# Keeping network products together between attention steps in the planned order of a fused attention and feed-forward kernel

## The chip, the cores and the metric

The kernel runs on one core of a Trainium2 chip. The metric is the device time of one execution in microseconds (us); before the change its median over 3 runs is 943.97 us (943.89 to 944.54).

## What is computed

Attention over q, k, v of 4 batches, 8 heads, 576 tokens and 64 columns, in two parts that are added: a softmax attention over tokens averaged in fours (its output repeated four times), and a local one in which a token sees tokens fewer than 4 places away. Its output, as 2304 tokens by 512 columns, goes through two feed-forward networks. The reference, cut:

```python
out_d = sm_attn(q_d, k_d, v_d)              # q, k, v averaged over 4 tokens
out_up = np.repeat(out_d, factor, axis=2)
scores = np.where(abs(i - j) < factor, scale * q @ k.T, -1e9)
attn_out = out_up + softmax(scores) @ v
g = x @ w_gate                              # 512 -> 1536
y = (g * sigmoid(g)) * (x @ w_val) @ w_out  # 1536 -> 512
h = np.maximum(y @ w_in, 0.0)               # 512 -> 2048
return h * h @ w_out2                       # 2048 -> 512
```

## The kernel before

Every engine executes its instructions in the order in which the program wrote them, and that order is not written by hand. A planner (class `Order`, its `run` and `next`) holds queues of tasks; a task is a chain of stages, each with an engine, a cost in planned us, the buffers that it takes and gives back, and a condition. The planner keeps a planned clock for each engine, looks which stages could start, and writes the instructions of the one that it picks (`s.fn()`), moving that engine's clock on. The chip then waits by semaphores wherever the plan was too early.

TensorE (PE) has two kinds of work.

**Attention steps.** Local attention has scores (L649, with L644 adding the mask in the first two batches), a transpose of the probabilities (L686) and the product with v (L707). Pooled ("global") attention has scores (L797), transposes (L816) and the product with v (L835). Between scores and transpose VectorE (DVE) and ScalarE (ACT) make a softmax; the transposed block is copied by ACT; the last product is read by ACT (L852) or added into a tile of x by DVE (L725). All of them write one of four PSUM banks with the tag `att`, used in turn. L649, L707, L797 and L835 use part of the 128 rows and columns of the array (the trace names them 64\*64, 64\*72 or 72\*64, and counts two records for each one of the program); L644 and L686 use 128\*128, L816 uses 72\*72.

**Network products.** A step is 12 matmuls of 128x128 weights with 256 tokens: four blocks of the depth, each as three products of high and low halves (`three`, L1045 to L1047). A unit of the first network is three steps, gate and value (into the two `gv` banks) and down (into `y`). Between value and down stands a chain: DVE L1094 multiplies, ACT L1100 makes the high half, DVE L1103 the low half of `hh`, which down reads. The second network follows, with products of blocks (L1045 to L1047 and L1980 to L1982), after all attention is done. The weights come in by DMA as raw bits and are taken apart by ACT and DVE (L367 to L384, L423, L426), in between.

Which kind PE takes next is decided in `next`: among PE's stages that could start within `LOOK_T` of the earliest, `rank` prefers attention (rank 0) to network products (rank 1) until attention steps in a row (`streak`) have used `ATT_MAX` planned us; then network products come first (rank -1). Attention stages are given `PE_MARGIN` of 0.1 us more than their inputs need.

Where a PE step that takes a bank is planned to wait over 0.6 us and the planned clock is between 40 and 100 us (or the step is a network product), `fill_bank` sets `pad`, and `bank` (L81) writes that many matmuls on zeros into the bank ahead of the step. Up to 40 us such matmuls are written by `fill` (L1251).

Of the kernel before, what the change touches and what calls it, by code (L numbers as in the profile page):

```python
# [63 lines left out]
def attn_moe_kernel(ctx: ExitStack, tc: tile.TileContext, qT, kT, vw, vin, vp, qp, kp, qs, ks, vs, maskc, masks, identc, wB, wC, out):  # L64
# [33 lines left out]
    def dma(size):  # L98
        return size / RATE

    AFTER = {"v": 0.15, "a": 0.2, "p": 0.2, "t": 0.25}
    ATT_MAX, LOOK_V, LOOK_A, LOOK_P, LOOK_T, LOOK_D, PE_MARGIN = 2.0, 0.1, 0.0, 0.2, 0.05, 0.6, 0.1
    PAD_END, PAD_WAIT, PAD_SHARE = 100.0, 0.6, 0.8
    TICK, FILL_END, BUSY = 10.24 / 3, 40.0, 3180
    W_DUE0, W_STEP, X_DUE0, X_STEP, X_STEP0 = 17.0, 2.2, 12.0, 20.0, 14.0
    S_DUE, S_STEP = 140.0, 15.0
    CUT_T, CUT_J, W_LAG, Q_LATE, Q_LATER, MASK_PE = 2, 4, 65.0, 10.0, 6.0, 2
    V_LATE, V_LATE1, V_LATE0, V_LEAD, W_LEAD, LEAD, LATE = -15.0, -10.0, -5.0, 1000.0, 1000.0, 80.0, 500.0
# [4 lines left out]
    class Stage:  # L113
        def __init__(self, engine, cost, fn, take=(), give=(), cond=None, share=1.0, late=0.0):
            self.engine, self.cost, self.fn, self.take, self.give, self.cond = engine, cost, fn, take, give, cond
            self.share, self.late = share, late
# [14 lines left out]
    class Order:  # L131
        def __init__(self):
            self.flying = []
            self.queues = {k: [] for k in ("x", "qk", "sum", "rows", "v", "att", "w", "mlp", "other", "done", "put")}
            n = {"att": N_ATT, "y": N_Y, "gv": N_GV, "p": N_P, "pt": N_PT, "v": N_V, "xt": N_XT}
            n |= {"sg": N_SG}
            self.free = {k: [0.0] * c for k, c in n.items()}
            self.named = {k: [(0.0, i) for i in range(n_[0])] for k, n_ in NAMED.items()}
            self.got = {k: [] for k in NAMED}
            self.clock = {e: 0.6 for e in "vaptd"}  # L140
            self.pad = 0
            self.load, self.filler, self.streak, self.landed = {}, None, 0.0, 0.0

        def hot(self, t):
# [59 lines left out]
        def next(self):  # L204

            found = {}
            heads = [(q[0], q) for q in self.queues.values() if q]
            for task, q in [(t, None) for t in self.flying] + heads:
                t = self.start(task)
                if t is None:  # L210
                    continue
                e = task.stages[task.at].engine
                if e is None:
                    return task, q, t, None
                wait = PE_MARGIN if e == "t" and not task.products else 0.0
                found.setdefault(e, []).append((max(t + wait, self.clock[e]), task, q, t))
            assert found, "no stage can go on"
            first = min(found, key=lambda e: min(c[0] for c in found[e]))
            limit = min(c[0] for c in found[first]) + LOOK[first]

            def rank(c):
                task = c[1]
                if task.products:
                    return (1 if first == "t" and self.streak < ATT_MAX else -1), task.due
                return 0, task.due

            _, task, q, t = min((c for c in found[first] if c[0] <= limit), key=rank)
            return task, q, t, first

        def run(self):  # L230
            while self.flying or any(self.queues.values()):
                task, q, t, engine = self.next()
                if q is not None:
                    q.pop(0)
                    self.flying.append(task)
                if task.at == 0:
                    self.flying += task.then
                s = task.stages[task.at]
                if engine == "t" and (task.products or self.clock["t"] >= FILL_END) and self.clock["t"] < PAD_END:
                    self.fill_bank(t, s)  # L240
                for k in s.take:
                    if k in self.named:
                        slot = min(self.named[k])
                        self.named[k].remove(slot)
                        self.got[k].append(slot[1])
                    else:
                        self.free[k].remove(min(self.free[k]))
                if engine == "t" and self.clock["t"] < FILL_END:
                    self.fill(max(t, self.clock["t"]), task)
                s.fn()  # L250
                if engine is not None:
                    c, cost = max(t, self.clock[engine]), s.cost
                    if engine == "t":
                        cost = self.columns(c, cost, s.share)
                        self.streak = 0.0 if task.products else self.streak + cost
                    self.clock[engine] = c + cost
                    t = c + cost + AFTER.get(engine, 0.0) + s.late
                    if engine == "d":

                        t = self.landed = max(c + FLIGHT, self.landed) + cost  # L260
                        self.clock["d"] = max(c + ISSUE, self.landed - AHEAD)
                        t += SLACK if c > FIRST else 0.3
                    if engine == "p":

                        self.landed = max(c + FLIGHT, self.landed) + dma(128 * HP * SD) * ACC
                        self.clock["d"] = max(self.clock["d"], self.landed - AHEAD)
                        t = max(t, self.landed + SLACK)
                task.ready = t
                task.times.append(t)
                task.at += 1  # L270
                for k in s.give:
                    if callable(k):
                        name, slot = k()
                        self.named[name].append((t, slot))
                    else:
                        self.free[k].append(t)
                if task.done:
                    self.flying.remove(task)
# [2164 lines left out]
```

## Time and profile before

| | |
|---|---|
| median of 3 runs | 943.97 us (943.89 to 944.54) |
| the profiled execution | 943.21 us, of which 941.4 us from the first to the last instruction |
| PE matmul busy | 931.3 us, 99% of the span, 8929 instructions |
| DVE busy | 758.2 us, 81% |
| ACT busy | 583.4 us, 62% |
| DMA | 183.82 MB, 195 GB/s on average |

Busy is the time in which an engine had at least one instruction; matmuls overlap, so PE can be busy all the time and still not start matmuls at its fastest. What a step costs is therefore read from the distance between the starts of two steps in the timeline. The chain of waits that ended last lies on PE for 96% of the span.

### The profile page before, as it was taken

The numbers are of one execution on the slowest core, as the hardware profiler recorded it, in microseconds if no ns is written. First come the engines' busy times: TensorE is split into PE (matmuls) and PEld (weight loads), VectorE is DVE, ScalarE is ACT, GpSimd is POOL, SyncE is SP. The second block draws the span as 40 slices with busy tenths as digits, with TensorE's granted clock in tenths as the row PEclk, the third lists the DMA queues.
The fourth block names the chain that finished last, engine by engine and source line by source line (L and its number), as shares of the span: only waits on it lengthen the run. The fifth ranks groups of instructions, "written<-read, shape, count | busy, mean of one in ns | idle before, by whom it ended". The sixth has DMA issues, their size and how long they took to land.

```text
span 941.4 us, 22569 instructions
## 1 busy us (share of the span) xinstructions
PE 931.3 (99%) x8929; PEld 906.5 (96%) x8929; DVE 758.2 (81%) x1875; ACT 583.4 (62%) x1368; POOL 23.8 (3%) x31
## 2 busy tenths in 40 slices
PE   8999999999999999999999999999999999999997
PEld 7888999999999999999999999999999999999997
DVE  7998979778977788888896999968777667786775
ACT  4878566757666888466543575757565645445553
POOL 0102102000000000000000000000000000000000
PEclk9999999999999999999999999999999999999999
DMA  9998969485788756167462638614414864516131
GB/s 303 258 292 217 255 166 261 158 295 155 254 284 279 245 177 238 65 224 223 169 210 75 235 132 316 236 74 171 146 57 179 315 228 175 180 67 247 46 134 68
DMA packets 101205, 183.82 MB, mean 195 GB/s; under 512 B 22380, under 2 KB 60012, under 8 KB 101100
## 3 DMA queue, kind: packets, MB, share of 16 engines
q1 hardware_dynamic: 97644, 174.42, 54.7%
q0 software_dynamic: 3456, 7.96, 4.8%
q8 instruction: 70, 1.15, 0.5%
q14 instruction: 35, 0.29, 0.1%
HBM read 120.75 MB, written 61.60 MB: 194 GB/s over the span
## 4 chain that ended last, share of the span: by engine, by line
PE 96%; DVE 2%; ACT 1%; issue 0%; DVEq 0%
PE gv L1045 11%; PE gv L1046 11%; PE gv L1047 11%; PE y L1045 8%; PE y L1046 8%; PE y L1047 8%; PE att L1982 6%; PE att L1981 6%; PE att L1980 6%; PE att L1046 3%; PE att L1047 3%; PE att L1045 3%; PE att L707 2%; PE att L649 2%; PE att L797 2%; PE y L1251 2%
## 5 line engine op out<-in xcount | busy, mean ns | idle before, releaser
L1045 PE MATMUL gv<-xs,wg 128*128 128x256 f32 x880 | 250.5, 285 | 0.1
L1046 PE MATMUL gv<-xs,wg 128*128 128x256 f32 x880 | 247.0, 281 | 0.0
L1047 PE MATMUL gv<-xs,wg 128*128 128x256 f32 x880 | 246.8, 280 | 0.0
L1045 PEld LDWEIGHTS gv<-xs,wg 128*128 128x128 f32 x880 | 166.2, 189 | 2.3 <-DVE sg L1089 0.4
L1047 PEld LDWEIGHTS gv<-xs,wg 128*128 128x128 f32 x880 | 166.0, 189 | 0.0
L1046 PEld LDWEIGHTS gv<-xs,wg 128*128 128x128 f32 x880 | 166.0, 189 | 0.0
L2131 ACT ACTIVATE f<-rr 128x512 fp32r<-128x512 f32 (+2 forms) x200 | 87.8, 467 | 68.2 <-PE att L1982 32.2
L1982 PE MATMUL att<-wg,f 128*128 128x256 f32 x432 | 122.5, 284 | 0.5 <-DVE f L2134 0.4
L1980 PE MATMUL att<-wg,f 128*128 128x256 f32 x432 | 121.7, 282 | 0.3 <-ACT f L2131 0.3
L1981 PE MATMUL att<-wg,f 128*128 128x256 f32 x432 | 122.0, 282 | 0.0
L2134 DVE TENSOR_TENSOR f<-rr,f 128x512 fp32r<-128x512 f32 (+2 forms) x200 | 94.6, 490 | 29.5 <-ACT f L2131 28.4
L2055 ACT ACTIVATE rr<-rr 128x512 f32<-128x512 f32 (+1 forms) x144 | 79.8, 556 | 36.8 <-DVE rr L2058 35.0
L1046 PE MATMUL y<-xs,wg 128*128 128x256 f32 x336 | 94.7, 282 | 1.1 <-DVE xs L1570 1.1
L1045 PE MATMUL y<-xs,wg 128*128 128x256 f32 x336 | 94.6, 281 | 0.0
L1047 PE MATMUL y<-xs,wg 128*128 128x256 f32 x336 | 94.3, 281 | 0.0
L1982 PEld LDWEIGHTS att<-wg,f 128*128 128x128 f32 x432 | 81.2, 188 | 1.4 <-DVE f L2134 1.3
L1980 PEld LDWEIGHTS att<-wg,f 128*128 128x128 f32 x432 | 81.8, 189 | 0.6 <-ACT f L2131 0.6
L1981 PEld LDWEIGHTS att<-wg,f 128*128 128x128 f32 x432 | 81.5, 189 | 0.0
L2140 DVE TENSOR_TENSOR rr<-rr 128x256 f32<-128x256 f32 (+1 forms) x160 | 62.6, 393 | 9.1 <-ACT rr L2055 7.1
L1046 PEld LDWEIGHTS y<-xs,wg 128*128 128x128 f32 x336 | 63.5, 189 | 1.5 <-DVE xs L1570 1.5
L1045 PEld LDWEIGHTS y<-xs,wg 128*128 128x128 f32 x336 | 63.6, 189 | 0.4 <-ACT ys L1228 0.2
L1047 PEld LDWEIGHTS y<-xs,wg 128*128 128x128 f32 x336 | 63.5, 189 | 0.0
(149 smaller groups left out, 2316.8 us busy)
## 6 DMA issues: line engine op xcount, KB each, us to landing
wst<-wB SPq DMA_DIRECT2D x36, 512.0 KB, 5.0
w_sp<-tmp SPq DMA_DIRECT2D x36, 512.0 KB, 3.6
wg<-w_sp SPq DMA_DIRECT2D x36, 512.0 KB, 4.9
wst<-wC SPq DMA_DIRECT2D x32, 512.0 KB, 5.2
y_sp<-ys SPq DMA_DIRECT2D x29, 512.0 KB, 4.5
xf_sp<-xs SPq DMA_DIRECT2D x24, 512.0 KB, 2.7
xs<-xf_sp SPq DMA_DIRECT2D x24, 512.0 KB, 5.8
ys<-y_sp SPq DMA_DIRECT2D x20, 512.0 KB, 6.8
```

The costliest lines, as they stand in the source:

```text
L649: nc.tensor.matmul(u["s"][r, c * HP + hp], q[r, hp, q0 - o : q0 - o + WIN], k[r, hp, w0 - o : w0 - o + WIN], start=not mask_pe, stop=not m ...
L707: nc.tensor.matmul(ps[rr, o : o + t1 - t0], u["v"][rr, bls[c], hpp, h2, :], pt[rr, c, hpp, h2, t0 - q0 : t1 - q0], start=True, stop=True,)
L1045: nc.tensor.matmul(o, w[:, 0], x[:, 0], start=start, stop=False, skip_group_check=more)
L1046: nc.tensor.matmul(o, w[:, 0], x[:, 1], start=False, stop=False, skip_group_check=more)
L1047: nc.tensor.matmul(o, w[:, 1], x[:, 0], start=False, stop=stop, skip_group_check=more)
L1980: nc.tensor.matmul(o, h, w[:, 0], start=first and not again and c == 0, stop=False, skip_group_check=again)
L1981: nc.tensor.matmul(o, h, w[:, 1], start=False, stop=False, skip_group_check=again)
L1982: nc.tensor.matmul(o, l, w[:, 0], start=False, stop=end, skip_group_check=again)
L2055: return lambda: nc.scalar.activation(out=whole(f, c0), in_=whole(f, c0), func=func)
L2131: nc.scalar.activation(out=fac(k, 0), in_=source(), func=AF.Copy)
L2134: nc.vector.tensor_tensor(out=fac(k, 1), in0=source(), in1=fac(k, 0).bitcast(F32), op=ALU.subtract)
L2140: go = lambda: nc.vector.tensor_tensor(out=o(), in0=a(), in1=b(), op=op)
```

## The change

The planner gets three constants and two variables. `mode` remembers the kind of PE's last step: a step of the other kind is charged `SWITCH` = 0.1 planned us. `stay` adds up the planned time of network products since the last attention step; from 100 planned us on, while it is under `STAY` = 4.0 us (three steps of 1.41), a network product ranks before attention. `ATT_MAX` goes from 2.0 to 4.0 us. Nothing that is computed changes.

```diff
-    ATT_MAX, LOOK_V, LOOK_A, LOOK_P, LOOK_T, LOOK_D, PE_MARGIN = 2.0, 0.1, 0.0, 0.2, 0.05, 0.6, 0.1
+    ATT_MAX, LOOK_V, LOOK_A, LOOK_P, LOOK_T, LOOK_D, PE_MARGIN = 4.0, 0.1, 0.0, 0.2, 0.05, 0.6, 0.1
+    SWITCH, STAY, STAY_FROM = 0.1, 4.0, 100.0
...
-            self.pad = 0
+            self.pad, self.stay, self.mode = 0, 0.0, False
...
                 if task.products:
-                    return (1 if first == "t" and self.streak < ATT_MAX else -1), task.due
+                    stay = self.stay < STAY and self.clock["t"] > STAY_FROM and self.streak == 0.0
+                    return (1 if first == "t" and self.streak < ATT_MAX and not stay else -1), task.due
...
                     if engine == "t":
+                        c += SWITCH * (self.mode != task.products)
+                        self.mode = task.products
                         cost = self.columns(c, cost, s.share)
+                        self.stay = self.stay + cost if task.products else 0.0
                         self.streak = 0.0 if task.products else self.streak + cost
```

The order of all engines moves. Lines of the kernel after the change are 5 higher (L1050 for L1045). PE has 7380 rows of instructions before and 7336 now; the 44 that are gone are 22 of the 28 fillers of L81, each a weight load and a matmul. The other PE steps are the same in number. The first 352 rows of PE and the last 5317 stand as before, and on the queue of the DMAs (SP) 28 and 201 of 368; the last attention step is among the rows that moved. Before, 57 stretches of network steps lie between attention steps, now 42.

**Around the third down step of the first network, on PE** (`gv` is written by gate and value, `y` by down). Before, in a row:

```order
L1046 MATMUL gv<-xs,wg 128x256
L1047 MATMUL gv<-xs,wg 128x256
L797 MATMUL att<-kd,qd 72x144 x4
L816 MATMUL att<-ident,p 72x72 x4
L81 LDWEIGHTS zeros
L81 MATMUL gv<-zeros 128x256
```

With the change:

```order
L1051 MATMUL gv<-xs,wg 128x256
L1052 MATMUL gv<-xs,wg 128x256
L802 MATMUL att<-kd,qd 72x144 x4
L1050 MATMUL y<-hh,wg 128x256
L1051 MATMUL y<-hh,wg 128x256
L1052 MATMUL y<-hh,wg 128x256
```

Before, 15 such fillers and then the value step follow, then L797, L707 and the down step. Now the value step stands above, and only one attention step is left between it and its down step, with no filler.

**The same place on DVE**, from the product of gate and value (`sg`) to the low half of `hh`. Before:

```order
L588 TENSOR_TENSOR p<-p,rc 72x288
L1094 SCALAR_TENSOR_TENSOR sg<-sg,gv 128x256
L379 SCALAR_TENSOR_TENSOR wf<-wst,bits 128x512
L426 TENSOR_TENSOR wg<-wf,wg 128x512
L1103 TENSOR_TENSOR hh<-sg,hh 128x256
```

With the change:

```order
L560 TENSOR_SCALAR mx<-mx 72x2
L1099 SCALAR_TENSOR_TENSOR sg<-sg,gv 128x256
L431 TENSOR_TENSOR wg<-wf,wg 128x512
L384 SCALAR_TENSOR_TENSOR wf<-wst,bits 128x512
L1108 TENSOR_TENSOR hh<-sg,hh 128x256
```

Two passes over weights stand inside this chain in both orders.

**In the third batch's attention, on PE.** Before, in a row:

```order
L1047 MATMUL y<-hh,wg 128x256
L816 MATMUL att<-ident,p 72x72 x8
L649 MATMUL att<-kT,qT 64x64 x16
L835 MATMUL att<-pt,vd 64x72 x4
L1045 MATMUL gv<-xs,wg 128x256
```

With the change:

```order
L1052 MATMUL gv<-xs,wg 128x256
L840 MATMUL att<-pt,vd 64x72 x4
L821 MATMUL att<-ident,p 72x72 x4
L654 MATMUL att<-kT,qT 64x64 x16
L840 MATMUL att<-pt,vd 64x72 x4
L821 MATMUL att<-ident,p 72x72 x4
L654 MATMUL att<-kT,qT 64x64 x16
L821 MATMUL att<-ident,p 72x72 x4
L840 MATMUL att<-pt,vd 64x72 x4
L1050 MATMUL y<-hh,wg 128x256
```

Where four attention steps (L816 twice) stood between two network steps, with one network step behind them, eight stand now, with three behind; the eight use each of the four `att` banks twice.

## Rows read from the trace of the kernel before

**Rows 1.** The page: busy time by engine, and the granted clock in slices.

```profile
PE 931.3 (99%) x8929; PEld 906.5 (96%) x8929; DVE 758.2 (81%) x1875; ACT 583.4 (62%) x1368; POOL 23.8 (3%) x31
...
PEclk9999999999999999999999999999999999999999
```

**Rows 2.** Waits of PE: line and who ended it, us in total, times, longest.

```profile
PE y L1251 <- ACT zeros L1245: 2.4, 1, 2.4
...
PE att L835 <- ACT pt L822: 0.2, 1, 0.2
```

**Rows 3.** Busy time in stretches, us: PE, PEld, DVE, ACT, POOL, clock, DMA share, GB/s.

```profile
60.00:70.00 10.00, 9.98 (x115) 8.83 (x114) 9.68 (x25) 8.28 (x26) 0.00 (x0) 1.00 0.94 295
...
100.00:150.00 50.00, 49.98 (x674) 46.69 (x671) 40.71 (x109) 33.73 (x98) 6.94 (x8) 1.00 0.82 208
...
200.00:270.00 70.00, 69.91 (x906) 65.97 (x905) 60.56 (x153) 46.66 (x115) 0.00 (x0) 1.00 0.71 231
```

**Rows 4.** Timeline of PE (start us, us, engine, line), network steps among themselves.

```profile
340.49 0.28 PE L1045 MATMUL gv<-xs,wg 128*128 128x256 f32 x1
...
341.90 0.28 PE L1045 MATMUL y<-hh,wg 128*128 128x256 f32 x1
```

**Rows 5.** Timeline of PE, 129 to 136 us: both kinds by turns.

```profile
129.63 0.36 PE L1045 MATMUL gv<-xs,wg 128*128 128x256 f32 x1
...
131.23 0.47 PE L835 MATMUL att<-pt,vd 72*64 72x72 f32 x8
131.63 0.44 PE L816 MATMUL att<-ident,p 72*72 72x72 f32 x4
132.00 0.71 PE L797 MATMUL att<-kd,qd 64*72 64x144 f32 x8
132.65 0.44 PE L816 MATMUL att<-ident,p 72*72 72x72 f32 x4
132.89 0.36 PE L1045 MATMUL y<-hh,wg 128*128 128x256 f32 x1
...
134.50 0.72 PE L835 MATMUL att<-pt,vd 72*64 72x72 f32 x16
135.15 0.45 PE L816 MATMUL att<-ident,p 72*72 72x72 f32 x4
```

**Rows 6.** Timeline of PE: a network step that a transpose follows, twice.

```profile
80.76 0.38 PE L1045 MATMUL gv<-xs,wg 128*128 128x256 f32 x1
...
82.28 0.67 PE L816 MATMUL att<-ident,p 72*72 72x72 f32 x8
...
184.87 0.36 PE L1045 MATMUL y<-hh,wg 128*128 128x256 f32 x1
...
186.37 0.49 PE L686 MATMUL att<-ident,p 128*128 128x128 f32 x3
```

**Rows 7.** The chain that ended last, fillers in it: start us, us, what.

```profile
2.38 5.40 PE y L1251 x26
...
53.85 0.87 PE att L81 x7
...
61.41 1.64 PE gv L81 x15
...
68.36 0.66 PE gv L81 x6
```

**Rows 8.** Timeline of all engines, 64 to 67 us: end of a value step to its down step.

```profile
64.20 0.28 PE L1047 MATMUL gv<-xs,wg 128*128 128x256 f32 x1
...
64.52 0.42 DVE L1094 SCALAR_TENSOR_TENSOR sg<-sg,gv 128x256 f32<-128x256 f32 x1
...
65.46 0.69 DVE L426 TENSOR_TENSOR wg<-wf,wg 128x512 fp32r<-128x512 f32 x1
...
66.53 0.19 PEld L1046 LDWEIGHTS y<-hh,wg 128*128 128x128 f32 x1 [0.22 <-DVE hh L1103]
```

**Rows 9.** Timeline: local scores, and the DVE pass that sets their bank free.

```profile
145.03 1.15 PE L649 MATMUL att<-kT,qT 64*64 64x64 f32 x32
...
147.87 0.41 DVE L661 SCALAR_TENSOR_TENSOR p<-att,mask 128x256 f32<-128x256 f32 x1
```

## Prediction

> **What bounds the kernel now.** I read the page first. PE has a matmul under way for 99% of the span, at the full granted clock in every slice [rows 1]. The waits of PE say the same: after the first 2.4 us, the largest wait of the attention part is one of 0.2 us [rows 2]. So what counts is how closely PE's matmuls follow each other, and the stretches show DVE behind it with little room while attention runs: 9.68 of 10 us from 60 to 70, some 81 to 87% later [rows 3]. For PE I then went to the timeline and measured steps from start to start. A network step among its own kind takes 1.41 us [rows 4]. Between two attention steps it takes 1.60 (129.63 to 131.23) [rows 5], and 1.52 or 1.50 where a transpose (L816, L686) follows [rows 6]. So entering network work costs about 0.10, and leaving it for a step on part of the array (L649, L707, L797, L835; small steps below) another 0.08; leaving it for a transpose costs nothing. The same rows show that attention pays among itself: four L816 transposes take 0.37 when L797 follows and 0.24 when a network step does (from 131.63 and from 132.65) [rows 5], so a change from transposes to a small step costs about 0.13. A small step costs something by itself: L835 takes 0.40 with 8 records and 0.65 with 16 [rows 5], so 0.15 is per step and not per matmul.
>
> **The change, part by part.** Nothing is added or removed but 22 fillers; everything else is order. Times are against the profiled execution, 943.21 us, which lies 0.76 under the median.
>
> *1. Fewer stretches: -1.3.* I counted borders in the two orders. Entries into network work fall from 58 to 43: 15 x 0.11 = -1.65. Exits from it to a small step fall from 39 to 30: 9 x 0.08 = -0.72. But the attention steps now stand beside each other: changes from transposes to a small step rise from 14 to 21, 7 x 0.13 = +0.9, and there is one small stretch more (78 for 77), +0.15. Sum -1.3. The bounds: -0.1 if only the borders of small steps cost (their sum is 142 before and 141 now), and -2.9 if each of 15 stretches gave back the whole 1.60 - 1.41 = 0.19.
>
> The Trainium skill (TensorEngine Tiling (Array Packing), Key Properties) says that a change of tiling mode, and not a change of tile alone, drains TensorE. By that rule this term would be the -0.1. The trace agrees that the small steps' borders cost, but a step entered from and left to L686 transposes, full-array work on both sides, still takes 1.50 (from 184.87) [rows 6], so it is not the whole of it here.
>
> *2. Fillers: -2.5.* The 28 fillers of L81 take 0.87 + 1.64 + 0.66 = 3.17 us, 0.113 each [rows 7]; 22 x 0.113 = 2.5. They stood where the planner expected PE to wait; what waits come in their place is counted in 3 and 4. The bound on the other side is there, too.
>
> *3. A down step with nothing before it: +1.1.* In the changed order the third down step follows its value step after one L797 only. In the trace that chain takes 2.33 us: the value's last matmul starts at 64.20, the down step's second matmul, the first to need the low half of `hh`, at 66.53, after DVE had two passes over weights inside the chain, one of them the 0.69 of L426 [rows 8]. DVE's new order has the same two passes there. PE has to put between them 0.12 for that last matmul, about 0.75 for L797 with its border and 0.12 for the first down matmul: 1.0. So PE stands about 1.3 us; the 0.22 that the same step waits today [rows 8] goes, +1.1 net. Without the two passes the chain would be 1.3 shorter and the wait nothing; with two more passes in DVE's queue, 2.7. Behind the waiting step on PE stands all the rest of the order, so it counts in full.
>
> *4. Attention steps closer together: +0.9.* Eight in a row go round the four `att` banks twice, so a step may come to a bank that DVE has not read yet. Laying the steps' times from the rows along both orders (an estimate), I find seven places nearer to their producer than any such place before: three behind scores L649 (1.8, 1.9 and 2.1 us after their end, before at least 2.6), two behind masks L644 and transposes L686 (2.0 and 1.3, before 2.8 and 2.3), and two products right behind their transposes (0.65 and 1.28, before 1.08 and 1.56). If all waited until their old distance, that would be 4.6 us; if DVE and ACT are simply earlier, nothing. One row tells how far a release can lag: the DVE pass that frees a bank of the scores at 145.03 ends at 148.28, at least 2.1 us after the scores do [rows 9]. By that the three places of L649 wait 0.5 together; to the other four, most of which ACT releases, the less busy engine, I give a sixth of their 2.4, hence 0.9 in all.
>
> *5. The wait of L835 [rows 2] loses its place: -0.2.*
>
> At nothing I cost the rest. After the last attention step PE's 5317 rows are the same, in the same order, so what is gained by then stays gained; attention ends with 99 network steps ahead of it instead of 102. SP issues the same 368 rows; between the first 28 and the last 201 its loads of q, k, v, raw weights and its stores are moved past each other by a few places. Their cover is that the DMA engines are busy for 71 to 82% from 100 us on [rows 3]; at 60 to 70 it is 94%, and a late load there would show as a wait of L797 or of a value step. POOL's three accumulating loads of v and of pooled keys move by a place too and wait for attention steps anyway.
>
> Sum: -1.3 - 2.5 + 1.1 + 0.9 - 0.2 = -2.0: 943.21 becomes 941.2, and on the scale of the median **942.0 us**. A measurement of this kernel can tell about 0.2%, 1.9 us, from no change, so the forecast lies near that bound.
>
> **Rivals.**
>
> *Only small borders cost.* Then grouping gains 0.1 and not 1.3: 943.2 us. For it: the 0.13 that transposes pay before a small step is as much as an entry into network work, and the small borders hardly fall. Against: the 1.50 between transposes. This is also the case in which the change does not do what it says: fewer changes of kind, as many costly borders. It is what the skill's rule above would make of it.
>
> *Slower: DVE does not keep up with attention in blocks.* At the third down step two more DVE passes stand in the chain (2.7 - 0.2 = +2.5), and all seven near places wait their whole shortfall, +4.6: -1.3 - 2.5 + 2.5 + 4.6 = +3.3, 947.3 us. It decides once new waits pass 5.7 us (1.9 over the 3.8 of terms 1 and 2). For it: DVE is busy 9.68 of 10 us where the first comes [rows 3]. Against: later DVE has an eighth to a fifth of its time free, and eight steps are followed by three network steps, 4.2 us, in which it can catch up.
>
> *More is given back.* Each stretch gives 0.19 (-2.85), the fillers were all waste (-2.5), the down step waits 0.4 instead of 1.3 (+0.2), no other wait comes, and that of L835 goes (-0.2): -5.3, 938.6 us. For it: PE never waited at the fillers' ends, so they may have been longer than the waits. Against: [rows 8].
>
> *The clock falls.* An unfilled wait might cost the full clock. The first 26 fillers, behind the opening wait, took 5.40 us, 0.21 each, against 0.11 later [rows 7]: the lower of the two levels. As long a stretch again would cost 2.5: 944.5. Against: the granted clock is full everywhere else.
>
> **How the numbers follow.** Forecast 0.46, only small borders 0.17, slower 0.17, more given back 0.17, clock 0.03. Faster by over 0.2%: six tenths of the forecast's chance (its terms leave it some 1.2 us either way) and the third rival, 0.28 + 0.17 = 0.45. Slower: the second rival but for its mild end, with a little of the clock's, 0.17 rounded. The rest, 0.38, within 0.2%. The range takes in the third rival and the lower half of the slower case: 938.4 to 945.9 us.
>
> **What would show it.** L81 with 6 fillers. Network steps still 1.60 between L816 and L835, the sum of the stretches' excess over 1.41 per step lower by about 2.4 us, part of it found again in longer transposes. A wait of PE for DVE's `hh` of about 1.3 us some 60 us into the run, and waits of 0.2 to 0.5 behind scores near 155, 162 and 228 us. From the last attention step on, equal distances. The forecast is wrong if attention ends over 3 us earlier or no earlier relative to the network steps done, or if DVE's `hh` is not what PE waits for.

## The result and the profile after

The changed kernel takes 954.15 us (median of 4 runs, 953.2 to 956.0), the kernel before 943.93 us on the same chip: a ratio of 1.011 with an interval of [1.0092, 1.0128]. It is 1.1% slower; the forecast was 942.0 us and the range ended at 945.9, so both the sign and the range were wrong. The profiled execution took 953.2 us, 10.0 us more of span than the one before. Ratios leave out executions over 1.5% above the fastest of their kernel; there was one, of 2295.61 us, in the control below. (In `after`, and in the experiments made from it, lines behind the diff stand five higher: L1050 is the L1045 of before, L712 the L707.)

The page of the changed kernel: span, PE's busy time, and the granted clock in 40 slices.

```profile
span 951.4 us, 22531 instructions
...
PE 931.8 (98%) x8907; PEld 907.0 (95%) x8907; DVE 758.0 (80%) x1875; ACT 582.9 (61%) x1368; POOL 23.8 (2%) x31
...
PEclk9999999999989999999999999999999999999999
```

Against [rows 1], PE has 22 matmuls fewer (the fillers are gone, as planned) and is as long busy, but the span is longer, and one slice of the clock, the twelfth, is not full. PE's waits name the place; where before the largest wait of the attention part was 0.2 us [rows 2], there is now one of 6.0 us (waits of PE: line and who ended it, us in total, times, longest):

```profile
PE gv L1050 <- DVE sg L1099: 6.3, 2, 6.0
...
PE att L840 <- ACT pt L827: 1.7, 4, 0.8
...
PE y L1050 <- ACT hh L1105: 1.0, 1, 1.0
...
PE y L1051 <- DVE hh L1108: 0.6, 1, 0.6
```

The stretches show when (busy us of PE, PEld, DVE, ACT, POOL; then granted clock, DMA share, GB/s). First the kernel before, then the changed one, the last three rows around the long wait:

```profile
36.00:100.00 64.00, 63.75 (x846) 56.67 (x844) 59.51 (x163) 51.70 (x150) 10.38 (x12) 1.00 0.93 263
100.00:265.00 165.00, 164.82 (x2022) 155.98 (x2019) 139.01 (x365) 108.26 (x283) 9.54 (x11) 1.00 0.75 219
265.00:300.00 35.00, 35.00 (x319) 34.64 (x319) 27.60 (x60) 24.83 (x51) 0.00 (x0) 1.00 0.90 312
```

```profile
36.00:100.00 64.00, 60.99 (x840) 53.48 (x840) 59.51 (x162) 52.64 (x149) 11.28 (x13) 1.00 0.97 267
100.00:265.00 165.00, 164.12 (x1975) 155.77 (x1970) 137.72 (x364) 106.85 (x281) 8.64 (x10) 1.00 0.73 209
265.00:300.00 35.00, 29.00 (x272) 28.64 (x271) 20.51 (x43) 17.47 (x35) 0.00 (x0) 0.90 0.73 255
...
276.00:278.00 2.00, 0.40 (x2) 0.41 (x3) 2.00 (x5) 2.00 (x5) 0.00 (x0) 0.54 0.02 6
278.00:283.00 5.00, 5.00 (x25) 5.00 (x25) 4.01 (x10) 3.65 (x9) 0.00 (x0) 0.50 0.66 201
283.00:290.00 7.00, 7.00 (x62) 7.00 (x62) 4.03 (x10) 3.70 (x8) 0.00 (x0) 1.00 0.95 309
```

PE stands for 3.01 us between 36 and 100 (before 0.25), for 0.88 between 100 and 265 (0.18), and for 6.00 between 265 and 300 (0). Behind the 6.00 the granted clock is at 0.50, the lower of the two levels, until 283.

**Where the 10.0 us lie.** Two marks divide the span: the first network step and the end of the last attention step (L707, L712). Timeline of PE (start us, us, engine, line, in brackets the idle time before and what ended it), before and after:

```profile
36.25 0.38 PE L1045 MATMUL gv<-xs,wg 128*128 128x256 f32 x1
...
268.69 1.14 PE L707 MATMUL att<-pt,vw 64*64 64x58 f32 x32
269.76 0.38 PE L1045 MATMUL gv<-xs,wg 128*128 128x256 f32 x1
```

```profile
36.69 0.39 PE L1050 MATMUL gv<-xs,wg 128*128 128x256 f32 x1
...
265.10 2.08 PE L712 MATMUL att<-pt,vw 64*64 64x58 f32 x64
267.10 0.38 PE L1050 MATMUL y<-hh,wg 128*128 128x256 f32 x1
...
271.31 0.28 PE L1052 MATMUL gv<-xs,wg 128*128 128x256 f32 x1
277.60 0.58 PE L1050 MATMUL gv<-xs,wg 128*128 128x256 f32 x1 [6.00 <-DVE sg L1099]
```

Up to the first network step 0.44 us are lost; that start varies by more than this by itself (37.44 us in the kernel before without its fillers, below, whose order up to there is that of before). Between the marks lie 233.51 us with 102 network steps before and 230.41 us with 99 after; less 1.41 us for each step [rows 4] that is 89.69 and 90.82, so +1.13. From the second mark to the end there are 671.64 us before (941.4 - 269.76) and 684.30 after; less the three steps more that are then left to do (4.23) it is **+8.43**. The sum is 10.0.

**What PE waits for at 277.60.** The timeline of the other engines at that place, in the changed kernel:

```profile
266.29 0.64 DVE L730 TENSOR_TENSOR xt<-att,g 128x464 f32<-128x464 f32 x1 [1.61 <-PE att L712]
267.22 0.64 DVE L730 TENSOR_TENSOR xt<-att,g 128x464 f32<-128x464 f32 x1 [0.29 <-PE att L712]
267.78 0.68 DVE L1363 TENSOR_TENSOR tmp<-wf,tmp 128x512 fp32r<-128x512 f32 x1
275.32 1.89 DVE L1024 TENSOR_TENSOR xs<-xt,xs 128x512 fp32r<-128x512 f32 x3 [6.86 <-ACT xs L1020]
277.13 0.41 DVE L1099 SCALAR_TENSOR_TENSOR sg<-sg,gv 128x256 f32<-128x256 f32 x1
...
274.65 2.19 ACT L1020 ACTIVATE xs<-xt 128x512 fp32r<-128x512 f32 x4 [8.67 <-DMA x_sp<-xt]
...
268.49 0.32 SPq L450 DMA_DIRECT2D w_sp<-tmp x1
268.86 2.01 SPq L1211 DMA_DIRECT2D x_sp<-xt x2
```

Read it backwards. PE has two `gv` banks, and both are full; DVE L1099 frees one, but stands on DVE behind L1024, which waits 6.86 us for ACT L1020, which waits 8.67 us for a DMA. L1020 writes the high half of x for the first block behind attention, and it is the first instruction that writes into memory that attention has used: when all attention is done the planner's function `late` (L1300) releases attention's pool of buffers and opens a second one, `post`, in the same place. The first write to `post` must wait until everything that used the old pool has ended, the transfers out of it included. One buffer of the old pool is slot 5 of `tmp`, in which converted weights wait to be stored in `w_sp`; the planner may use it until attention is done (`apart("tmp", 5, turned_all)`, L1326). Its last filling is DVE L1363 at 267.78, behind the two adds L730, and its store goes out at 268.49. The profile names another store, of x to `x_sp`, issued just after it; which of the two it is, the experiments had to say.

In the kernel before the same store went out with the two at 263.58, and the first write to `post` was ACT L1354 at 270.74, which waited for DVE only:

```profile
263.58 2.05 SPq L445 DMA_DIRECT2D w_sp<-tmp x2
...
270.74 0.94 ACT L1354 ACTIVATE tmp<-wf 128x512 fp32r<-128x512 f32 x2 [1.07 <-DVE xt L725]
```

### The profile page after: what moved, and what is told of

The parts are those of the page before. It is cut to its first block, busy times and chain, and to the rows that moved or that the text cites. A ratio compares the mean times of both kernels' runs of the same rounds, so it can differ in the third digit from the quotient of the medians.

```text
span 951.4 us, 22531 instructions
## 1 busy us (share of the span) xinstructions
PE 931.8 (98%) x8907; PEld 907.0 (95%) x8907; DVE 758.0 (80%) x1875; ACT 582.9 (61%) x1368; POOL 23.8 (2%) x31
## 4 chain that ended last, share of the span: by engine, by line
PE 87%; DVE 6%; ACT 4%; DMA 1%; issue 1%; SPq 0%; DVEq 0%; ACTq 0%
PE gv L1050 10%; PE gv L1051 10%; PE gv L1052 10%; PE y L1050 8%; PE y L1051 8%; PE y L1052 8%; PE att L1987 6%; PE att L1986 6%; PE att L1985 6%; PE att L1051 3%; PE att L1052 3%; PE att L1050 3%; PE att L802 2%; PE att L712 1%; PE y L1256 1%; PE att L654 1%
## 5 line engine op out<-in xcount | busy, mean ns | idle before, releaser
L1050 PE MATMUL gv<-xs,wg 128*128 128x256 f32 x880 | 249.7, 284 | 6.5 <-DVE sg L1099 6.3
L1050 PEld LDWEIGHTS gv<-xs,wg 128*128 128x128 f32 x880 | 166.9, 190 | 8.0 <-DVE sg L1099 6.8
L1050 PE MATMUL y<-xs,wg 128*128 128x256 f32 x336 | 94.6, 281 | 0.1
L1051 PEld LDWEIGHTS y<-xs,wg 128*128 128x128 f32 x336 | 63.5, 189 | 1.5 <-DVE xs L1575 1.5
L1050 PE MATMUL y<-hh,wg 128*128 128x256 f32 x216 | 63.3, 293 | 1.0 <-ACT hh L1105 1.0
L1050 PEld LDWEIGHTS y<-xs,wg 128*128 128x128 f32 x336 | 63.6, 189 | 0.4 <-ACT ys L1233 0.3
```

What stands on the lines that cost most here:

```text
L1050: nc.tensor.matmul(o, w[:, 0], x[:, 0], start=start, stop=False, skip_group_check=more)
L1051: nc.tensor.matmul(o, w[:, 0], x[:, 1], start=False, stop=False, skip_group_check=more)
```

## The experiments

**Theory A**: the release of attention's pool waits for the last store of slot 5; PE stands 6.0 us for it, and the idle time brings the lower clock, some 2.5 us more; the rest, 1 to 1.5 us, is the attention part. **Rivals**: the stores of x are what is waited for, or x is late (B); the clock has nothing to do with the idle time (C); the attention part itself is what costs (D).

**Slot 5 given up early.**

```diff
-late_ = Task([apart("tmp", 5, turned_all), apart("bits", 1), Stage(None, 0.0, late)])
+late_ = Task([apart("tmp", 5, lambda: 0.0 if order.clock["t"] > 245.0 else None),
+              apart("bits", 1, turned_all), Stage(None, 0.0, late, cond=turned_all)])
```

Expected: 

> The changed kernel, but slot 5 of tmp (the buffer whose last store to w_sp starts late, L450) is given up from 245 us of the plan on, so that nothing written to the second pool after attention waits for a store to w_sp. Theory A (the release of the attention pool waits for the store of slot 5; PE then stands for 6.0 us and runs at half clock for 6.83 us): the wait of 6.0 us on the gv bank and the half clock go, about 954.2 - 6.0 - 2.5 = 945.7 us (944.7 to 946.7). Rival B (what is waited for is the store of x_sp, as the row of the profile names it, or x itself is late because the last two steps of L712 now stand together): the x_sp stores and the L712 steps are as they were, so the wait and the time stay, 953 to 955 us.

Measured: 945.84 us, ratio to before 1.0011 [1.0001, 1.0021]. The stretch behind attention:

```profile
266.00:290.00 24.00, 24.00 (x223) 23.93 (x220) 18.55 (x40) 17.85 (x36) 0.00 (x0) 1.00 0.95 354
```

PE does not stand at all from 266 to 290, the clock is full, and the time is the 945.7 that theory A gave. B falls in both forms: the last two L712 steps stand together here too.

**The stores of x moved behind the release.**

```diff
+def stored_x():
+    return whole() if t < NT1 - 2 else after([late_]) if whole() is not None else None
-spill_ = Task([Stage("d", dma(128 * 4 * n), spill, cond=whole)])
+spill_ = Task([Stage("d", dma(128 * 4 * n), spill, cond=stored_x)])
```

Expected: 

> The changed kernel, but the last two stores of x to x_sp (L1211) are issued only after the attention pool has been released; the last store of tmp slot 5 to w_sp stays ahead of it. Theory A: the writer of the second pool still waits for the w_sp store, PE stands for 4 to 7 us behind DVE sg L1099 and the time is 952 to 956 us. Rival B (the x_sp stores are what is waited for): the wait goes and the time is 945 to 947 us.

Measured: 953.45 us, ratio 1.0091 [1.0076, 1.0106]. Now that the stores of x are out of the way, the timeline of ACT names the other:

```profile
276.73 2.19 ACT L1020 ACTIVATE xs<-xt 128x512 fp32r<-128x512 f32 x4 [8.24 <-DMA w_sp<-tmp]
```

PE stands 5.67 us in this trace, which is of the slowest of the four executions (954.77 us). The wait belongs to the store of `tmp`; the name in the changed kernel's row was the wrong one of two stores under way at that moment.

**The wait filled.** 48 products between the second and the third gv step:

```diff
+def cover(w, x):
+    n_gv[0] += 1
+    if n_gv[0] == 69:
+        o = bank("att")[:, :256]
+        for _ in range(16):
+            three(o, w[:, :, :128], x[0][:, :, 0, :256], True, True)
...
 proj(u["g"], w_tiles[j, 0], xh_t[name, ti], n)
+cover(w_tiles[j, 0], xh_t[name, ti])
```

(and the same behind the value's `proj`). Expected: 

> The changed kernel with 48 products of 128x256 on operands that are loaded already, into a free bank of the att tag, between the second and the third gv step after attention, where PE stands idle for 6.0 us; at 0.117 us each they take 5.6 us of it and nothing reads them. Theory A: the wait for the store is unchanged (the third gv step starts at 277.6 us of the span), but PE has not been idle, the granted clock stays at 1.0 and the 2.3 to 2.7 us that the 6.83 us at half clock cost are saved: 951.2 to 952.2 us. Rival C (the lower clock has nothing to do with that idle time, or its loss is made up later): 954 us as the changed kernel.

Measured: 951.04 us, ratio 1.0068 [1.0052, 1.0084]. The same step of PE, and the stretch that was at 0.50:

```profile
277.84 0.39 PE L1050 MATMUL gv<-xs,wg 128*128 128x256 f32 x1 [0.31 <-DVE sg L1108]
...
276.00:283.00 7.00, 6.69 (x57) 6.49 (x56) 6.91 (x16) 6.43 (x15) 0.00 (x0) 1.00 0.44 140
```

The step starts 0.24 us later than in the changed kernel, so the wait for the store is untouched; the clock stays full. From that step to the end of the span there are 671.4 us here and 673.8 in the changed kernel: 2.4 us is what the lower clock cost. C falls. Six microseconds for the store and 2.4 for the clock are the 8.43, to within 0.1.

**Control: slot 5 given up early in the kernel before.** The same edit. Expected: 

> Control: the kernel before the change with the same early end of tmp slot 5 at 245 us of the plan. In the kernel before, the last store from slot 5 had landed before the first write to the second pool, so giving up the slot should take nothing away: 943.5 to 944.5 us by every theory. If it gains 1 us or more, part of what the first run gains is not the wait that the change brought.

Measured: 948.73 us (median of four executions; the fifth is the 2295.61 named above), ratio 1.0039 [1.0025, 1.0053], a miss for every theory. It gains nothing, so giving up the slot is no gain by itself, and what it gained in the changed kernel was the new wait; but it loses 0.4%. The planner puts everything behind the edit into another order, and 116 us behind the last attention step PE waits 2.16 us for ACT with a lower clock behind it (timeline of PE; a stretch):

```profile
388.14 0.38 PE L1045 MATMUL att<-h,wg 128*128 128x256 f32 x1 [2.16 <-ACT h L1804]
...
388.00:391.00 3.00, 2.79 (x16) 2.59 (x17) 2.64 (x7) 1.54 (x4) 0.00 (x0) 0.78 0.19 35
```

An edit of the order is thus worth some us either way at places far behind it. What releases ACT so late there was not tried.

**The parts alone.** One of the three parts of the change each, in the changed kernel's code:

```diff
-SWITCH, STAY, STAY_FROM = 0.1, 4.0, 100.0      # ATT_MAX = 4.0
+SWITCH, STAY, STAY_FROM = 0.1, 0.0, 100.0      # ATT_MAX = 2.0: SWITCH alone
+SWITCH, STAY, STAY_FROM = 0.0, 4.0, 100.0      # ATT_MAX = 2.0: STAY alone
+SWITCH, STAY, STAY_FROM = 0.0, 0.0, 100.0      # ATT_MAX = 4.0: ATT_MAX alone
```

SWITCH alone, expected: 

> One part of the change alone: the charge of 0.1 for each change of kind (SWITCH = 0.1, STAY = 0, ATT_MAX = 2.0). 56 attention stretches instead of 58, 11 fillers instead of 28. Theory A (the time goes where the release of the attention pool waits for the last store of tmp slot 5): this store is written 21 instructions ahead of the first write to the second pool, against 14 in the changed kernel, and the last L712 step stands alone, so the wait is shorter, 2 to 5 us, and 946 to 951 us. Rival D (what costs is the attention part itself, its waits and its longer blocks): blocks are as in the kernel before, so 942 to 944 us.

STAY alone, expected: 

> One part alone: TensorE keeps to network products for at least 4.0 us between attention steps (STAY = 4.0, SWITCH = 0, ATT_MAX = 2.0). 51 stretches, 28 fillers as before. Theory A: the store of slot 5 is written 17 instructions ahead of the first write to the second pool, so most of the wait is there, 4 to 6 us, partly at half clock: 949 to 955 us. Rival D: its attention blocks are no longer than before, 943 to 945 us.

ATT_MAX alone, expected: 

> One part alone: attention may go on for up to 4.0 us (ATT_MAX = 4.0, SWITCH = 0, STAY = 0). 53 stretches, 32 fillers. Theory A: the store of slot 5 is written 66 instructions ahead of the first write to the second pool and has landed by then, so there is no wait there and no half clock: 943 to 946 us. Rival D (longer blocks starve the engines): this part has the longer blocks and would have most of the loss, 948 to 954 us.

Measured: 954.88 us, ratio 1.0102 [1.0081, 1.0124]; 953.39 us, 1.0081 [1.0066, 1.0096]; 947.82 us, 1.0025 [1.0015, 1.0035]. The first write to `post` on ACT, and the step of PE behind it where it waits, for SWITCH, for STAY and for ATT_MAX:

```profile
280.19 0.63 ACT L1359 ACTIVATE tmp<-wf 128x512 fp32r<-128x512 f32 x1 [7.04 <-DMA w_sp<-tmp]
...
282.53 0.58 PE L1050 MATMUL gv<-xs,wg 128*128 128x256 f32 x1 [5.15 <-DVE sg L1099]
```

```profile
288.10 1.15 ACT L1020 ACTIVATE xs<-xt 128x512 fp32r<-128x512 f32 x2 [6.70 <-DMA w_sp<-tmp]
...
289.61 0.58 PE L1050 MATMUL y<-hh,wg 128*128 128x256 f32 x1 [3.96 <-ACT hh L1105]
```

```profile
275.49 2.20 ACT L1020 ACTIVATE xs<-xt 128x512 fp32r<-128x512 f32 x4 [0.23 <-DMA wst<-wC]
```

So the wait comes with SWITCH or with STAY, and not with the longer blocks: D, as a cause of the whole loss, falls, since the part that has the longer blocks loses least. It also falls that the two adjacent L712 steps make the store late, as I had thought from the changed kernel's rows: SWITCH and STAY alone end attention with a single L712 step and wait all the same. What goes with the wait, in these four orders, is how many instructions are written between the store and the first write to `post`: 14 in the changed kernel, 21 and 17 here, and 66 with ATT_MAX alone. Two of the three times lie outside what theory A gave. SWITCH is above its 951; its attention part is also 4.4 us longer than that of before, measured between the marks as above. So for SWITCH alone D is right about part of the loss. ATT_MAX is 1.8 above its 946 (and just under D's 948), and of its span's 6.4 us over the one before, 3.3 lie ahead of the first network step. Both traces are of the slowest execution, 957.51 and 949.6 us, which lie 2.6 and 1.8 above the medians; neither was followed further.

**The change from 100 us on, slot 5 given up.** SWITCH and ATT_MAX apply, as STAY does, only where the planned clock is past 100:

```diff
-c += SWITCH * (self.mode != task.products)
+c += SWITCH * (self.mode != task.products) * (self.clock["t"] > STAY_FROM)
-return (1 if first == "t" and self.streak < ATT_MAX and not stay else -1), task.due
+return (1 if first == "t" and self.streak < (ATT_MAX if self.clock["t"] > STAY_FROM else 2.0)
+        and not stay else -1), task.due
```

Expected: 

> All three parts, but only from 100 us of the plan on, and slot 5 given up at 245 us of the plan: 47 stretches, 28 fillers as before, the first 100 us as in the kernel before, no store of slot 5 ahead of the second pool. Theory A: no wait after attention (0.3 us at most) and none of the waits of the changed kernel at 64 to 86 us of the span; 11 stretches fewer at the price that the changed kernel shows (about 0.35 us in all) and the few small waits behind 100 us (0.2 to 0.5 us each) about cancel: 943.5 to 945.5 us. If borders cost what the prediction took for them (0.08 us a stretch or more) and the waits stay away: 942.5 to 943.5 us.

Measured: 944.76 us, ratio 1.0 [0.999, 1.0009]: as theory A had it, and no gain. (A wait of 0.73 us on a gv bank is left at 275.31, for DVE and not for a store; 0.3 at most was expected.) Eleven stretches fewer, with fillers and the first 100 us as before, give no gain in all. Between the marks this kernel is 1.07 us longer than before by the same reckoning, with 0.90 us of PE idle between 36 and 265 where before it was 0.43, so 0.4 to 0.6 us come from the order itself (a wait costs somewhat more than its idle time, as term 1 below shows). This does not say that borders are free: the same attention work is cut into more steps here, 76 small ones against 68 (counted in PE's rows). At the prediction's 0.15 for each the eight more take 1.2 us, and by that estimate the fewer borders gave some 0.7.

**Without the fillers.** In the kernel before, and in the last one:

```diff
-        for _ in range(order.pad):
+        for _ in range(0):
```

The kernel before, expected: 

> The kernel before the change without its 28 fillers (L81, products on zeros that nothing reads), 22 of which the change takes out; every other instruction stands as it was. Theory P (the prediction's term 2: nothing but the fillers ends in that time, so 22 of them are worth 2.5 us): 28 fillers of 0.113 us in mean go, 3.0 us, 941 to 943 us where the kernel before has 944 to 945. Theory C (the fillers cover waits on ACT and DVE that are there anyway; in the changed kernel PE stands for 3.0 us between 36 and 100 us of the span, where before it stood for 0.25): PE waits in their place, within 0.7 us of the kernel before, or slower if the granted clock falls.

The last one, expected: 

> The version with the change from 100 us of the plan on and slot 5 given up at 245 us (last batch: even with the kernel before), now without its 28 fillers too. Theory P: 3.0 us less, 941 to 943 us. Theory C: PE waits where the fillers stood, 944 to 946 us.

Measured: 943.96 us, ratio 0.9992 [0.9983, 1.0002], and 944.23 us, 0.9997 [0.9987, 1.0007]. Three microseconds less would be 0.9968, outside both intervals; by its ratio the first is 0.8 us below the kernel before, close to theory C's 0.7, and the second is in C's range. The stretch and PE's waits in it, the kernel before without its fillers:

```profile
36.00:100.00 64.00, 62.30 (x826) 55.06 (x822) 59.82 (x164) 52.41 (x150) 10.40 (x12) 1.00 0.96 266
...
62.44 0.39 PE L1045 MATMUL gv<-xs,wg 128*128 128x256 f32 x1 [0.52 <-ACT wg L423]
63.34 0.38 PE L1047 MATMUL gv<-xs,wg 128*128 128x256 f32 x1 [0.40 <-DVE wg L426]
69.34 0.38 PE L1047 MATMUL gv<-xs,wg 128*128 128x256 f32 x1 [0.35 <-DVE wg L426]
```

Both groups of fillers in a gv bank had stood before a step whose weights were not taken apart yet. Between the marks this kernel is 0.61 us shorter than before, for fillers that took 3.00 us from start to start. The clock stays full in this trace. (One of the ten executions of each of these two kernels has a mean granted clock of 0.997 and 0.998 and is the slowest, 946.93 and 947.5 us; no execution of the kernel before on that chip is below 0.999. No trace shows where it fell.) No version tried is faster than the kernel before by more than the measurement can tell; this one has the lowest ratio.

## Why the prediction was wrong

**The step that failed** is the sentence on the end: "After the last attention step PE's 5317 rows are the same, in the same order, so what is gained by then stays gained." That the order is the same is true. But an equal order on PE says nothing of when the other queues let it run, and I looked at PE's rows only, across the one place where a pool changes hands. I had counted SP's stores as moved "by a few places" and hidden because the DMA engines were not full; what mattered was the last user of one buffer against the first writer of the next pool. This gave +8.4 us where the prediction had 0.

**The clock.** The rival was priced rightly and thought too unlikely: 2.5 us for one stretch at the lower level, from the first fillers [rows 7], against 2.4 measured; its chance was 0.03. In the changed kernel's trace it came with the long wait for the store, not with the shorter waits that the rival had in mind.

**Term 1, fewer stretches: -1.3 predicted, about -1.4 measured.** Between the marks the change is +1.13; the fillers are 2.43 shorter (3.00 to 0.58 us, start to start), PE's idle time from 36 to 265 is 3.46 longer, and 0.1 seems to be left for the order. But a wait costs PE more than the idle time in its row, as three rows of one network step and the next show (changed kernel, timeline of PE):

```profile
261.42 0.28 PE L1052 MATMUL gv<-xs,wg 128*128 128x256 f32 x1
262.05 0.39 PE L1050 MATMUL gv<-xs,wg 128*128 128x256 f32 x1 [0.35 <-DVE sg L1099]
262.28 0.28 PE L1051 MATMUL gv<-xs,wg 128*128 128x256 f32 x1
```

From the first start to the third lie 0.86 us. Two such spacings without a wait take 0.24 (1.41 for twelve, [rows 4]), so 0.62 are lost at a wait of 0.35. I compared every step beside a wait with the same kind of step that has the same kind of neighbours and no wait, from start to start: the changed kernel's waits take 1.52 us beyond their idle time, those of before 0.06. So the new waits cost about 4.9 us and not 3.46, and what is left for the order is not 0.1 but some -1.4 (an estimate). The network steps gave back about 3.0 and the attention steps took 1.6 more, where I had 2.4 and about 1. Each part is off by 0.6, in opposite directions, so that the sum comes this close to -1.3 is partly luck. Seven more borders from transposes to a small step are there, as counted; six are of the short L821 kind, which the 0.13 was read from.

So the rival "only small borders cost" is not borne out in this kernel. The Trainium skill (TensorEngine Tiling (Array Packing), Key Properties) has it that a change of tiling mode drains TensorE. By that rule the term is -0.1; the -1.4 does not agree with it as the whole price.

**Term 2, fillers: -2.5 predicted.** The matmuls went as counted, 2.43 us. Their worth did not: 28 of them taken out alone shorten the attention part by 0.61, so 22 are worth about 0.5 in proportion (an estimate). I wrote that the waits that come in their place were counted in terms 3 and 4, and these covered only places that the new order makes tighter. The fillers also hid waits for weights on ACT and DVE, which [rows 2] cannot show, because a matmul on zeros fills them: without the fillers PE is idle for 1.46 us more between 36 and 265, and the waits take 0.8 beyond that by the comparison above.

**Terms 3 to 5, waits: +1.8 predicted, +3.46 of idle time and about +4.9 in all measured**, the waits from under the fillers among them. The third down step waits where the prediction said, 0.96 us for ACT's half of `hh` and 0.59 for DVE's, 1.55 against 1.3 for DVE's alone. Its chain was longer than I took it to be: DVE's L1099 starts at 63.33, 0.86 us after the value's last matmul (62.47), where L1094 took 0.32 before [rows 8]. The products of pooled attention, one of the near places of term 4, were under-priced:

```profile
64.36 0.38 PE L1050 MATMUL y<-hh,wg 128*128 128x256 f32 x1 [0.96 <-ACT hh L1105]
65.33 0.38 PE L1051 MATMUL y<-hh,wg 128*128 128x256 f32 x1 [0.59 <-DVE hh L1108]
...
74.89 0.47 PE L840 MATMUL att<-pt,vd 72*64 72x72 f32 x8 [0.41 <-ACT pt L827]
78.05 0.47 PE L840 MATMUL att<-pt,vd 72*64 72x72 f32 x8 [0.84 <-ACT pt L827]
```

Three of them stand 1.43 us together (the third 0.18, at 85.78), for ACT's copy of the transposed block, where I gave four such places 0.4. These five waits are nearly all of the 3.01 us from 36 to 100. Nearness was the right thing to look for. The slower rival (DVE behind in the blocks, new waits of over 5.7 us) did not come true as told: the waits stay under its price, and 2.39 of these 2.98 us end with ACT; how far DVE held ACT up there was not tried.

Without the pool's handover the sum would have been wrong by about 3 us still: the version without that wait stands at a ratio of 1.0011 [1.0001, 1.0021], 1 us above before where the forecast was 2 below. These 3 us are the waits of terms 2 to 5, taken at 1.8 and costing 4.9; either miss alone was enough to lose the sign.

## What to carry to other kernels

Where a program hands memory from one phase to the next, find for the old phase the last instruction or transfer that uses it and for the new one the first that writes it, and check the distance between the two in every new order, on all engines; an unchanged order behind that place proves nothing. Fillers, or other work that nobody waits for, are not worth their length: take them out alone and see what wait appears. Price a wait by the starts of the matmuls around it and not by its idle time alone, or a saving elsewhere will look like nothing. And before counting a border as a saving, price it by what stands on its two sides and count the steps, since regrouping may move borders or cut the work into more pieces.

## What was unexpected of the hardware

The granted clock went to its lower level at 276 us, near the end of 6.00 us without a matmul, although PE had been busy for over 190 us ahead of it without a gap of more than 0.35 us, and it was full again some 5.4 us after work began (277.60 to 283). It fell as well during or behind idle stretches of 5.67, 5.15, 3.96 and 2.16 us in four other kernels. Behind the waits of 0.96 and 0.59 us at the third down step it did not fall in the changed kernel's trace (1.00 from 36 to 100 us), but it did behind the same two waits in the version with the stores of x moved, whose order is the same up to there (timeline of PE; a stretch):

```profile
66.23 0.38 PE L1050 MATMUL y<-hh,wg 128*128 128x256 f32 x1 [0.96 <-ACT hh L1105]
67.20 0.38 PE L1051 MATMUL y<-hh,wg 128*128 128x256 f32 x1 [0.59 <-DVE hh L1108]
...
68.00:71.00 3.00, 3.00 (x38) 2.78 (x38) 2.50 (x9) 1.59 (x7) 0.00 (x0) 0.50 0.59 225
```

So the same short waits can be followed by the lower clock in one execution and not in another, and the clock rival of the prediction, an unfilled wait in the attention part, came true in part there. And the changed kernel's row named the store of x as what ended ACT's wait, while the store issued 0.37 us ahead of it was the one: with two transfers landing close together, a releaser in the profile is a suggestion, and moving one of them settles it.
